# Output strips of a quarter of the columns, and memory rows turned by VectorE, in a segment-recurrent attention block

## The chip, the cores and the metric

The kernel runs on one core of a Trainium2 chip. The metric is device time in microseconds (us) of one execution: the median of three runs, and one further execution is recorded by the hardware profiler. TensorE multiplies matrices, VectorE (DVE in the profile), ScalarE (ACT) and GpSimd (POOL) work on elements, SyncE (SP) issues DMA transfers.

## The reference

A pre-norm block: recurrent attention with 8 memory rows over segments of 32 tokens, then a feed-forward layer with squared ReLU. Batch 1, 2048 tokens, width 640, 32 heads of 128, feed-forward width 1728, bfloat16.

```python
idx = jnp.arange(L)                       # L = M + seg = 8 + 32
mask = (idx[:, None] < M) | (idx[:, None] >= idx[None, :])
mem = mem0
for s in range(n_seg):                    # 64 segments, one after the other
    h = jnp.concatenate([mem, xs], axis=1)            # xs: layernorm(x) of the segment
    q, k, v = (jnp.einsum('btd,dhe->bhte', h, W) for W in (Wq, Wk, Wv))
    scores = jnp.einsum('bhqe,bhke->bhqk', q, k) * scale
    scores = jnp.where(mask[None, None], scores, -1e9)
    o = jnp.einsum('bhqk,bhke->bhqe', softmax(scores), v)
    o = jnp.einsum('bhte,hed->btd', o, Wo)
    mem = o[:, :M, :]                     # the next segment needs these 8 rows
    outs.append(o[:, M:, :])
h = x + concatenate(outs)
out = h + (relu(layernorm(h) @ w1 + b1) ** 2) @ w2 + b2
```

## The kernel before

The 64 segments form a recurrence: step s cannot project its memory rows before step s-1 has produced them. A step works on 32 main rows (8 memory rows and the first 24 tokens, HD = 24) of all heads; the last 8 tokens of each segment ("tails", TL = 8) are projected ahead, four segments at a time, as filler work.

All matmuls of the loop use TensorE as four strips of 32 columns, each with a weight load of its own: four matmuls in a row write the four groups of 32 PSUM partitions. `proj` (L194) projects the 32 rows with 512 columns a matmul: 40 matmuls each for q, k and v in a step.

The order on TensorE is the order in which `step` (L368) writes it:

1. q, k, q, k projections (L450 to L470), with copies by ScalarE and 32 x 32 transposes by VectorE (`flip`, L224) into `qT` and `kT`. `kT` has 64 columns for a head: 32 main keys, and the 8 tail keys four times over, once for each of the four heads that share a group of score rows.
2. `scores(0)` (L401): memory rows against all keys for half of the heads. A mask matmul (L404) first writes -1e9 where a tail key belongs to another head, and 16 matmuls of 64 columns (L409) add the scores. `qz` holds the memory queries spread out with zeros, so that four heads accumulate into one tile.
3. The v projection in pieces, with `token_scores(0)`, `scores(1)` and `token_scores(1)` between them. Token scores (tile `sk`, L485, 40 columns) start with a causal mask by matmul (L481).
4. `soft1` and `soft2` (L413, L422): maximum, exponential, reciprocal, scaling and transpose for the memory rows, on VectorE and ScalarE.
5. One filler unit, then `token_values` of step s-1 and `values` of the memory rows, into tile `po`; `values_out` moves the memory rows to `oT`.
6. Two filler units, then the output product `wo_rounds` (L229): 64 matmuls of 320 columns. Strip j = 2 kh + ch holds half ch of the output columns for half kh of the heads. `wo_out` (L239) adds the two halves of the heads: ScalarE copies partitions 64 to 127 (L243), VectorE adds (L244), and `o` holds 64 rows of 320.
7. Five filler units, then `mem_to_hT` (L304): 20 matmuls against the identity (L308) turn the 8 memory rows so that the width lies on partitions, and VectorE copies them into `hT4` (L310), from which the next step's q projection reads. `tails_in` (L312) brings the next segment's tail queries and keys into `qT` and `kT`, on GpSimd.
8. The remaining filler.

The token softmax (L522 to L539) runs beside the output product: maximum, difference and sum on VectorE, exponential on ScalarE, two products on GpSimd (`pkt`, `pk`), two transposes on VectorE at the step's end; its result is used by the next step's `token_values`.

Filler units come from lists (`fill`): a tail projection unit has 4 matmuls of 512 columns (10 units a step in most steps); every fourth step the 10 units are instead the tail rows' output product (`wo_tail_units`, L285). In a few steps the list is short or empty. `late`, `mid` and `win` hold work of other engines, such as layer norm, for set places. PSUM has three `mm` tiles, one `ch` tile (scores, output product and turned memory rows take turns in it) and the `po` tile.

Of the kernel before, what the change touches and what calls it, by code (L numbers as in the profile page):

```python
# [16 lines left out]
def kernel(  # L17
# [16 lines left out]
    nc = tc.nc  # L34
# [9 lines left out]
    DH = D // 2  # L44
    NB = S // 128
# [36 lines left out]
    mask = const.tile([128, HG, SEG], BF16)  # L82
    nc.vector.memset(mask[:], 0.0)
    nc.gpsimd.affine_select(out=mask[0:32], in_=mask[0:32], compare_op=ALU.is_ge, fill=NEG, base=0,
                            pattern=[[0, HG], [-1, SEG]], channel_multiplier=1)
    bmask = const.tile([128, 4, TL], BF16)
# [10 lines left out]
    nc.vector.tensor_scalar(out=bmask[:], in0=same[:], scalar1=-1.0, scalar2=-NEG, op0=ALU.add, op1=ALU.mult)  # L97
    qT = const.tile([128, H, NK], BF16)
    kT = const.tile([128, H, 2 * SEG], BF16)
# [28 lines left out]

    o_ring = [const.tile([128, DH], BF16, name="o%d" % k) for k in range(5)]
    for o in o_ring:  # L130
        nc.gpsimd.memset(o[64:128], 0.0)
    o0 = o_ring[-1]
    nc.vector.memset(o0[0:64], 0.0)
    load_x(0)
    for ch in range(2):
        nc.sync.dma_start(out=o0[32 * ch:32 * ch + M, :].rearrange("m (c f) -> m c f", f=64),
                            in_=A_mem0[0].rearrange("m (c t f) -> t m c f", t=2, f=64)[ch])
# [89 lines left out]
    wov2 = wo[:].rearrange("p h (c t f) -> p h t c f", t=2, f=64)  # L227

    def wo_rounds(lhs, pw, h0, h1):  # L229

        for h in range(h0, h1):
            for kh in range(2):
                for ch in range(2):
                    j = kh * 2 + ch
                    p = h // 8 * 16 + kh * 8 + h % 8
                    nc.tensor.matmul(pw[32 * j:32 * j + 32, 0:DH], lhsT=lhs(p), rhs=wov2[:, head(p), ch],  # L236
                                     start=(h == 0), stop=(h == 15))

    def wo_out(pw):  # L239
        o = o_ring[0]  # L240
        o_ring.append(o_ring.pop(0))
        tmp = s1.tile([128, DH], F32, tag="tk", name="otmp")
        nc.scalar.copy(out=tmp[0:64], in_=pw[64:128, 0:DH])  # L243
        nc.vector.tensor_tensor(out=o[0:64], in0=pw[0:64, 0:DH], in1=tmp[0:64], op=ALU.add)  # L244
        return o
# [39 lines left out]
    def wo_tail_units(b):  # L285
        st = {}

        def out():
            o = wo_out(st["ps"])
            dst = o_all[:].rearrange("(b s t) d -> b s t d", s=4, t=SEG)  # L290
            for ch in range(2):
                nc.sync.dma_start(out=dst[b, :, HD:SEG, ch * DH:(ch + 1) * DH], in_=o[32 * ch:32 * ch + 32, :])

        def unit(k):
            def f():
                if k == 0:
                    st["ps"] = mmtile()
                wo_rounds(lambda p: oTts[b % 2][:, p, :], st["ps"], k * 16 // 10, (k + 1) * 16 // 10)
                if k == 9:
                    late.append(out)  # L300
            return f
        return [unit(k) for k in range(10)]

    def mem_to_hT(o, hT4, sp):  # L304
        pm = chn.tile([128, 512], F32, tag="ch", name="pm")
        for c in range(DC):
            for q in range(4):
                nc.tensor.matmul(pm[32 * q:32 * q + 32, c * M:(c + 1) * M], lhsT=o[:, (2 * c + q % 2) * 32:(2 * c + q % 2 + 1) * 32],  # L308
                                 rhs=ident[:, q // 2 * 32:q // 2 * 32 + M], start=True, stop=True)
        nc.vector.tensor_copy(out=hT4[:, :, sp, 0:M], in_=pm[:, 0:DC * M].rearrange("p (c m) -> p c m", m=M))  # L310

    def tails_in(b, sp):  # L312
        q, k = [tails[b][w][:].rearrange("p h (k s) -> p h s k", s=4)[:, :, sp, :] for w in "qk"]
        nc.gpsimd.tensor_copy(out=qT[:, :, SEG:NK], in_=q)
        nc.gpsimd.tensor_copy(out=kT[:, :, SEG:2 * SEG].rearrange("p h (j k) -> p h j k", k=TL),  # L315
                              in_=k.unsqueeze(2).to_broadcast([128, H, 4, TL]))
# [11 lines left out]
    def store_main(o, s):  # L328
        for ch in range(2):
            nc.sync.dma_start(out=o_all[s * SEG:s * SEG + HD, ch * DH:(ch + 1) * DH],  # L330
                              in_=o[32 * ch + M:32 * ch + 32, :])
# [36 lines left out]
    def step(b, sp, v=None):  # L368
# [32 lines left out]
        def scores(n):  # L401
            sm = chn.tile([128, 512], F32, tag="ch", name="sm")
            for g in range(G):
                nc.tensor.matmul(sm[32 * g:32 * g + 32, SEG:2 * SEG], lhsT=ident[:, 0:32],  # L404
                                 rhs=bmask[:].rearrange("p j k -> p (j k)"), start=True, stop=False, skip_group_check=True)
            for j in range(4):
                for g in range(G):
                    p = n * 16 + g * 4 + j
                    nc.tensor.matmul(sm[32 * g:32 * g + 32, 0:2 * SEG], lhsT=qz[:, p, :], rhs=kT[:, p, :],  # L409
                                     start=False, stop=(j == 3), skip_group_check=True)  # L410
            sms[n] = sm

        def soft1(n):  # L413
            mx = s2.tile([128, 1], F32, tag="mx", name="mx")
            nc.vector.tensor_reduce(out=mx[:], in_=sms[n][:, 0:2 * SEG], op=ALU.max, axis=AX.X, negate=True)  # L415
            em = s2.tile([128, 2 * SEG], BF16, tag="em", name="em")
            zm = s2.tile([128, 1], F32, tag="zm", name="zm")
            nc.scalar.activation(out=em[:], in_=sms[n][:, 0:2 * SEG], func=ACT.Exp, bias=mx[:, 0:1], scale=1.0,  # L418
                                 accum_out=zm[:])
            ems[n], zms[n] = em, zm  # L420

        def soft2(n):  # L422
            rm = s2.tile([128, 1], F32, tag="rm", name="rm")
            nc.vector.reciprocal(out=rm[:], in_=zms[n][:])
            pm = s2.tile([128, 2 * SEG], BF16, tag="pmem", name="pmem")
            nc.vector.tensor_scalar(out=pm[:], in0=ems[n][:], scalar1=rm[:, 0:1], scalar2=None, op0=ALU.mult)
            pT = s2.tile([128, 2 * SEG], BF16, tag="pTm", name="pTm")
            nc.vector.transpose(out=pT[:], in_=pm[:])
            return pT
# [42 lines left out]
        if not ready:  # L472
            ps0 = mmtile()
            proj(wv, "half", lhs, 0, ps0, 0, 2)
        sk = mmtile()
        skv = sk[:, 0:HG * NK].rearrange("p (i k) -> p i k", k=NK)

        def token_scores(n):
            if n == 0:
                for g in range(G):  # L480
                    nc.tensor.matmul(skv[32 * g:32 * g + 32, :, M:NK], lhsT=ident[:, 0:32], rhs=mask[:],  # L481
                                     start=True, stop=False, skip_group_check=True)
            for j in range(4):
                for g in range(G):
                    nc.tensor.matmul(skv[32 * g:32 * g + 32, n * 4 + j, :], lhsT=qT[:, n * 16 + g * 4 + j, M:NK],  # L485
                                     rhs=kT[:, n * 16 + g * 4 + j, 0:NK], start=False, stop=(n == 1 and j == 3),
                                     skip_group_check=True)

        token_scores(0)
        if not ready:  # L490
            proj(wv, "half", lhs, 0, ps0, 2, DC)
            nc.scalar.copy(out=v[:, 0:512], in_=ps0[:])  # L492
        if not last:
            pT0 = soft2(0)
        if not ready:
            ps1 = mmtile()
            proj(wv, "half", lhs, 1, ps1, 0, 2)
        if not last:
            scores(1)
        token_scores(1)  # L500
        if not ready:
            proj(wv, "half", lhs, 1, ps1, 2, DC)
# [4 lines left out]
        if not ready:  # L507
            nc.scalar.copy(out=v[:, 512:1024], in_=ps1[:])
        run(fill, 10 if ready else 1)
# [13 lines left out]
        nc.vector.tensor_reduce(out=mxk[:], in_=skv, op=ALU.max, axis=AX.X)  # L523
        tk = s1.tile([128, HG, NK], F32, tag="tk", name="tk")
        nc.vector.tensor_tensor(out=tk[:], in0=skv, in1=mxk[:].unsqueeze(2).to_broadcast([128, HG, NK]), op=ALU.subtract)  # L525
        ek = s1.tile([128, HG, NK], BF16, tag="ek", name="ek")
        nc.scalar.activation(out=ek[:], in_=tk[:], func=ACT.Exp, scale=1.0)  # L527
        for f in outs:
            f()
        zk = s1.tile([128, HG], F32, tag="zk", name="zk")  # L530
# [9 lines left out]

        pw = chn.tile([128, 512], F32, tag="ch", name="pw")
        wo_rounds(lambda p: oT[:, p, 0:32], pw, 0, 16)
# [5 lines left out]
        if not last:  # L548
            run(fill, 5)
            mem_to_hT(o, hT4s[(s + 1) // 4], (s + 1) % 4)  # L550
            tails_in((s + 1) // 4, (s + 1) % 4)
# [69 lines left out]
    def prep_sum(t, k, got):  # L621
        ot, fx = got
        fv = fx.rearrange("p (c t f) -> p t c f", t=2, f=64)
        nc.vector.tensor_tensor(out=fv, in0=ot.rearrange("p (t c f) -> p t c f", t=2, f=64), in1=fv, op=ALU.add)
# [81 lines left out]
    mem_to_hT(o0, hT4s[0], 0)  # L706
# [54 lines left out]
    def end_output(s):  # L761
        pw = chn.tile([128, 512], F32, tag="ch", name="pw")
        wo_rounds(lambda p: oT[:, p, 0:32], pw, 0, 16)
# [108 lines left out]
```

## Time and profile before

| | |
|---|---|
| median of 3 runs | 1040.74 us (1040.04 to 1044.46) |
| span of the profiled execution, first to last instruction | 1035.5 us |
| mean granted TensorE clock | 0.993 |
| from the first q projection of step 1 to that of step 63 | 70.18 to 886.12 us |
| TensorE matmuls, busy | 26960, 980.1 us (95%) |
| VectorE, ScalarE, GpSimd busy | 621.6, 536.0, 312.3 us |
| output product L236 of the steps | 4224 matmuls, 300 ns mean |
| turning the memory rows L308 | 1280 matmuls |

A busy time is the union of the instructions' intervals on one engine. Matmuls are pipelined: the mean of one is its whole passage, while four strips start within some nanoseconds of each other, so a stretch of matmuls is read from its start times. In a group, "out<-in" names the tiles, the shape is partitions x elements, and the idle time is that of the engine before the group's instructions, with what ended it; "issue" means that nothing the profile shows was waited for. The median lies 5.2 us above the span.

### The profile page before, as it was taken

Reading aid. Unit: us, or ns where it says so; the run is one execution under the profiler, and the core shown is the slowest. Engines: PE = TensorE matmul, PEld = TensorE weight load, DVE = VectorE, ACT = ScalarE, POOL = GpSimd, SP = SyncE. Lnnn points to the kernel's source line nnn. Section 1 sums busy time; section 2 is a strip of 40 time slices with the busy share of each in tenths; the row PEclk is TensorE's granted clock in tenths of the full one; section 3 lists DMA queues with packets and bytes.
Section 4 is the critical chain, followed back from the end, with each engine's and each line's share of the span. In section 5 each row is a group of like instructions: output and inputs, shape, how many; then the busy total and the mean of one; then the engine's idle time right before and its main releaser. Section 6 shows DMA issues by size and latency. Waiting matters only on the chain.

```text
span 1035.5 us, 58905 instructions
## 1 busy us (share of the span) xinstructions
PE 980.1 (95%) x26960; PEld 563.9 (54%) x26960; DVE 621.6 (60%) x1740; ACT 536.0 (52%) x1225; POOL 312.3 (30%) x805
## 2 busy tenths in 40 slices
PE   5879899999999999999999999999999998999998
PEld 2335455555655555555555655555555555555565
DVE  2155666766566666666666666666666676565432
ACT  2435555555555555555555555555555555534431
POOL 1033333333333333332333233333333333343210
PEclk9889999999999999999999999999999999999999
DMA  8960101000100000000000000000000110612200
GB/s 319 405 205 26 22 7 31 7 24 6 32 10 22 15 24 24 16 20 14 26 15 22 15 27 15 22 15 27 15 21 8 47 33 7 194 54 72 77 26 26
DMA packets 39112, 51.58 MB, mean 50 GB/s; under 512 B 6160, under 2 KB 34960, under 8 KB 36944
## 3 DMA queue, kind: packets, MB, share of 16 engines
q1 hardware_dynamic: 38000, 47.30, 13.8%
q8 instruction: 210, 3.44, 1.4%
q14 instruction: 38, 0.31, 0.1%
q10 hardware_dynamic: 544, 0.26, 0.1%
q0 software_dynamic: 320, 0.26, 0.1%
HBM read 38.37 MB, written 9.44 MB: 46 GB/s over the span
## 4 chain that ended last, share of the span: by engine, by line
PE 83%; DMA 6%; DVE 5%; issue 3%; ACT 2%; POOL 0%; SPq 0%; DVEq 0%; ACTq 0%; POOLq 0%
PE ps L204 45%; PE pw L236 13%; PE y L823 6%; PE ps L791 5%; PE ps L236 3%; DMA xt<-in_A_x_dram 3%; PE po L437 2%; PE pm L308 2%; PE sm L409 2%; DMA wq<-in_B_w_dram 1%; PE po L343 1%; PE ps L485 1%; ACT em L418 1%; DMA vt_d<-row 1%; DVE o L244 1%
## 5 line engine op out<-in xcount | busy, mean ns | idle before, releaser
L204 PEld LDWEIGHTS <-hT 128*32 128x32 bf16 x7680 | 186.9, 96 | 180.8 <-DVE hT L310 19.6
L204 PE MATMUL ps<-wv,hT 128*32 128x512 bf16 x2520 | 169.9, 379 | 0.7 <-ACT v L492 0.7
L236 PE MATMUL pw<-wo,oT 128*32 128x320 bf16 x4224 | 159.6, 300 | 3.3 <-DVE pTt L555 1.2
L204 PE MATMUL ps<-wq,hT 128*32 128x512 bf16 x2520 | 158.1, 380 | 4.8 <-DVE hT L310 4.8
L204 PE MATMUL ps<-wk,hT 128*32 128x512 bf16 x2520 | 157.6, 379 | 0.0
L236 PEld LDWEIGHTS <-oT 128*32 128x32 bf16 x4224 | 109.3, 97 | 50.7 <-DVE oT L211 15.8
L535 POOL TENSOR_TENSOR pkt<-ek,rk 128x64 bf16<-128x64 bf16 x64 | 18.8, 294 | 377.6 <-DVE rk L533 377.6
L220 ACT ACTIVATE row<-ps 128x512 bf16<-128x512 f32 x156 | 91.9, 601 | 78.4 <-PE ps L204 74.6
L225 DVE STREAM_TRANSPOSE qT<-row 128x512 bf16<-128x512 bf16 x128 | 90.6, 709 | 51.9 <-ACT row L220 51.9
L222 ACT CAST row<-ps 128x512 bf16<-128x512 f32 x115 | 65.9, 596 | 34.3 <-PE ps L204 34.3
L315 POOL COPY kT<-kTt 128x1024 bf16<-128x1024 bf16 x64 | 70.9, 1108 | 13.7 <-DVE kTt L225 13.7
L362 POOL COPY qz<-qT 128x96 bf16<-128x96 bf16 x126 | 33.4, 265 | 125.0 <-DVE qT L225 121.5
L353 ACT CAST oT<-po 128x512 bf16<-128x512 f32 x128 | 68.7, 589 | 1.6
L244 DVE TENSOR_TENSOR o<-pw,otmp 64x320 bf16<-64x320 f32 x66 | 31.8, 482 | 61.9 <-ACT otmp L243 61.9
L204 PEld LDWEIGHTS <-hTt 128*32 128x32 bf16 x1920 | 48.8, 99 | 35.6 <-issue 9.9
L225 DVE STREAM_TRANSPOSE kT<-row 128x512 bf16<-128x512 bf16 x65 | 46.0, 708 | 31.1 <-ACT row L222 31.1
L243 ACT COPY otmp<-pw 64x320 f32<-64x320 f32 x66 | 27.9, 422 | 70.9 <-PE pw L236 70.9
L823 PE MATMUL y<-wq,wk 128*128 128x320 bf16 x416 | 60.9, 299 | 0.0
L393 ACT CAST row<-ps 128x256 bf16<-128x256 f32 x126 | 40.7, 375 | 29.1 <-PE ps L204 29.0
L531 DVE TENSOR_REDUCE zk<-ek 128x8 f32<-128x320 bf16 x64 | 31.1, 486 | 40.2 <-ACT ek L527 40.2
L527 ACT ACTIVATE ek<-tk 128x320 bf16<-128x320 f32 x64 | 30.1, 470 | 45.1 <-DVE tk L525 45.1
L418 ACT ACTIVATE em<-sm,mx 128x64 bf16<-128x64 f32 x126 | 40.4, 321 | 24.3 <-DVE mx L415 24.3
(114 smaller groups left out, 1657.5 us busy)
## 6 DMA issues: line engine op xcount, KB each, us to landing
wv<-in_A_Wv_dram SPq DMA_DIRECT2D x5, 1024.0 KB
wq<-in_A_Wq_dram SPq DMA_DIRECT2D x5, 1024.0 KB
wk<-in_A_Wk_dram SPq DMA_DIRECT2D x5, 1024.0 KB
wo<-in_A_Wo_dram SPq DMA_DIRECT2D x4, 1280.0 KB
vt<-vt_d SPq DMA_DIRECT2D x60, 64.0 KB
xt<-in_A_x_dram SPq DMA_DIRECT2D x20, 160.0 KB
vt_d<-row SPq DMA_DIRECT2D x22, 128.0 KB
wq<-in_B_w_dram SPq DMA_DIRECT2D x1, 2080.0 KB
```

The source lines that it names most:

```text
L204: nc.tensor.matmul(ps[32 * k:32 * k + 32, :], lhsT=lhs(c), rhs=wr[:, c, n, k], start=(c == 0), stop=(c == DC - 1))
L220: nc.scalar.mul(out=row, in_=ps, mul=scale)
L222: nc.scalar.copy(out=row, in_=ps)
L225: nc.vector.transpose(out=dst[:, n * 16:(n + 1) * 16, 0:32], in_=row.rearrange("p (h e) -> p h e", e=32))
L236: nc.tensor.matmul(pw[32 * j:32 * j + 32, 0:DH], lhsT=lhs(p), rhs=wov2[:, head(p), ch], start=(h == 0), stop=(h == 15))
L244: nc.vector.tensor_tensor(out=o[0:64], in0=pw[0:64, 0:DH], in1=tmp[0:64], op=ALU.add)
L315: nc.gpsimd.tensor_copy(out=kT[:, :, SEG:2 * SEG].rearrange("p h (j k) -> p h j k", k=TL), in_=k.unsqueeze(2).to_broadcast([128, H, 4, TL]))
L353: nc.scalar.copy(out=oTg[:, n, :, :, M:NK], in_=po[:, :, n * 128:(n + 1) * 128].rearrange("p g (j q) -> p g j q", q=32))
L393: nc.scalar.copy(out=row[:, u * 256:(u + 1) * 256], in_=ps[:, u * 256:(u + 1) * 256])
L418: nc.scalar.activation(out=em[:], in_=sms[n][:, 0:2 * SEG], func=ACT.Exp, bias=mx[:, 0:1], scale=1.0, accum_out=zm[:])
L791: nc.tensor.matmul(ps[:], lhsT=w1[:, c, fc * 128:(fc + 1) * 128], rhs=hnT[:, c, :], start=(c == 0), stop=(c == DC - 1))
L823: nc.tensor.matmul(y[:, hh, 0:DH], lhsT=f1T[:, fc, k * 128:(k + 1) * 128], rhs=w2[:, fc, cs], start=(fc == 0), stop=False, skip_group_chec ...
```

## The change

- The output product is cut into four strips of 160 columns (`DQ`), one for each quarter of the output columns, over all 32 heads: 128 matmuls of 160 columns in place of 64 of 320. The sum of two halves falls away: `wo_out` is one ScalarE copy of 128 x 160. Stores of `o` become four DMAs in place of two, and `prep_sum` reads the new column order.
- `mem_to_hT` is a VectorE transpose of the product in PSUM (float32, 128 x 160) and a copy of 40 columns into `hT4`. It and `tails_in` stand right behind the output product, ahead of the token softmax's sum; all remaining filler comes later. For step 0 the memory rows are turned by 5 matmuls.
- The token mask is no longer written by matmul (L481): VectorE adds it to the scores ahead of the maximum, which adds one operation of 128 x 320.
- `kT` has 40 columns a head: tail keys are held once. The mask matmul L404 falls away, scores of the memory rows have 40 columns, and `soft2` spreads the tail probabilities with a second VectorE operation (a product with `same`).
- Token scores of both halves stand behind the v projection, and `scores(1)` behind its first 24 matmuls instead of the first 28.

```diff
-    def wo_rounds(lhs, pw, h0, h1):
-
-        for h in range(h0, h1):
-            for kh in range(2):
-                for ch in range(2):
-                    j = kh * 2 + ch
-                    p = h // 8 * 16 + kh * 8 + h % 8
-                    nc.tensor.matmul(pw[32 * j:32 * j + 32, 0:DH], lhsT=lhs(p), rhs=wov2[:, head(p), ch],
-                                     start=(h == 0), stop=(h == 15))
+    wov4 = wo[:].rearrange("p h (c q f) -> p h q c f", q=4, f=32)
+    def wo_rounds(lhs, pw, p0, p1):
+        for p in range(p0, p1):
+            for q in range(4):
+                nc.tensor.matmul(pw[32 * q:32 * q + 32, 0:DQ], lhsT=lhs(p), rhs=wov4[:, head(p), q],
+                                 start=(p == 0), stop=(p == H - 1))
     def wo_out(pw):
...
-        nc.scalar.copy(out=tmp[0:64], in_=pw[64:128, 0:DH])
-        nc.vector.tensor_tensor(out=o[0:64], in0=pw[0:64, 0:DH], in1=tmp[0:64], op=ALU.add)
+        nc.scalar.copy(out=o[:], in_=pw[:, 0:DQ])
...
-    def mem_to_hT(o, hT4, sp):
+    def mem_to_hT(pw, hT4, sp):
+        tr = s1.tile([128, DQ], F32, tag="tr", name="tr")
+        nc.vector.transpose(out=tr[:], in_=pw[:, 0:DQ])
+        nc.vector.tensor_copy(out=hT4[:, :, sp, 0:M], in_=tr[:].rearrange("p (c r) -> p c r", r=32)[:, :, 0:M])
...
-        nc.gpsimd.tensor_copy(out=kT[:, :, SEG:2 * SEG].rearrange("p h (j k) -> p h j k", k=TL),
-                              in_=k.unsqueeze(2).to_broadcast([128, H, 4, TL]))
+        nc.gpsimd.tensor_copy(out=kT[:, :, SEG:NK], in_=k)
...
         def scores(n):
             sm = chn.tile([128, 512], F32, tag="ch", name="sm")
-            for g in range(G):
-                nc.tensor.matmul(sm[32 * g:32 * g + 32, SEG:2 * SEG], lhsT=ident[:, 0:32],
-                                 rhs=bmask[:].rearrange("p j k -> p (j k)"), start=True, stop=False, skip_group_check=True)
             for j in range(4):
                 for g in range(G):
                     p = n * 16 + g * 4 + j
-                    nc.tensor.matmul(sm[32 * g:32 * g + 32, 0:2 * SEG], lhsT=qz[:, p, :], rhs=kT[:, p, :],
+                    nc.tensor.matmul(sm[32 * g:32 * g + 32, 0:NK], lhsT=qz[:, p, :], rhs=kT[:, p, :],
...
-            nc.vector.tensor_scalar(out=pm[:], in0=ems[n][:], scalar1=rm[:, 0:1], scalar2=None, op0=ALU.mult)
+            nc.vector.tensor_scalar(out=pm[:, 0:SEG], in0=ems[n][:, 0:SEG], scalar1=rm[:, 0:1], scalar2=None, op0=ALU.mult)
+            nc.vector.scalar_tensor_tensor(out=pm[:, SEG:2 * SEG].rearrange("p (j k) -> p j k", k=TL),
+                                           in0=ems[n][:, SEG:NK].unsqueeze(1).to_broadcast([128, 4, TL]),
+                                           scalar=rm[:, 0:1], in1=same[:], op0=ALU.mult, op1=ALU.mult)
...
-        token_scores(0)
         if not ready:
-            proj(wv, "half", lhs, 0, ps0, 2, DC)
+            proj(wv, "half", lhs, 0, ps0, 0, DC)
...
-            proj(wv, "half", lhs, 1, ps1, 0, 2)
+            proj(wv, "half", lhs, 1, ps1, 0, 1)
         if not last:
             scores(1)
-        token_scores(1)
         if not ready:
-            proj(wv, "half", lhs, 1, ps1, 2, DC)
+            proj(wv, "half", lhs, 1, ps1, 1, DC)
...
+        for i in range(HG):
+            for g in range(G):
+                p = i // 4 * 16 + g * 4 + i % 4
+                nc.tensor.matmul(skv[32 * g:32 * g + 32, i, :], lhsT=qT[:, p, M:NK], rhs=kT[:, p, 0:NK],
+                                 start=(i == 0), stop=(i == HG - 1), skip_group_check=True)
...
-        nc.vector.tensor_reduce(out=mxk[:], in_=skv, op=ALU.max, axis=AX.X)
-        nc.vector.tensor_tensor(out=tk[:], in0=skv, in1=mxk[:].unsqueeze(2).to_broadcast([128, HG, NK]), op=ALU.subtract)
+        nc.vector.tensor_tensor(out=tk[:], in0=skv, in1=mask[:].unsqueeze(1).to_broadcast([128, HG, NK]), op=ALU.add)
+        nc.vector.tensor_reduce(out=mxk[:], in_=tk[:], op=ALU.max, axis=AX.X)
+        nc.vector.tensor_tensor(out=tk[:], in0=tk[:], in1=mxk[:].unsqueeze(2).to_broadcast([128, HG, NK]), op=ALU.subtract)
...
+        pw = chn.tile([128, 512], F32, tag="ch", name="pw")
+        wo_rounds(lambda p: oT[:, p, 0:32], pw, 0, H)
+        if not last:
+            mem_to_hT(pw, hT4s[(s + 1) // 4], (s + 1) % 4)
+            tails_in((s + 1) // 4, (s + 1) % 4)
...
-        pw = chn.tile([128, 512], F32, tag="ch", name="pw")
-        wo_rounds(lambda p: oT[:, p, 0:32], pw, 0, 16)
         o = wo_out(pw)
...
-        if not last:
-            run(fill, 5)
-            mem_to_hT(o, hT4s[(s + 1) // 4], (s + 1) % 4)
-            tails_in((s + 1) // 4, (s + 1) % 4)
         run(mid, 2)
         run(fill, 100)
```

## The prediction

> **What bounds the kernel now.** I read the page first, then the chain of waits, then TensorE's timeline, then the instruction queue.
>
> ```profile
> PE 980.1 (95%) x26960; PEld 563.9 (54%) x26960; DVE 621.6 (60%) x1740; ACT 536.0 (52%) x1225; POOL 312.3 (30%) x805
> ...
> q8 instruction: 210, 3.44, 1.4%
> ```
>
> TensorE looks full. The second line, from the table of DMA queues, matters more than it seems: 3.44 MB in 210 packets is 16,384 bytes a packet, and 2 x 26960 instructions over 210 packets is 257 each. So TensorE's program arrives in blocks of 256 instructions, which is 128 pairs of weight load and matmul.
>
> The end of a step, from the chain of waits (start, duration, what):
>
> ```profile
> 329.15 2.27 PE pw L236 x64
> ...
> 331.49 0.43 ACT otmp L243
> ...
> 331.94 0.49 DVE o L244
> ...
> 332.48 0.35 PE pm L308 x20
> ...
> 332.86 0.21 DVE hT L310
> ...
> 333.12 4.50 PE ps L204 x80
> ```
>
> The output product begins at 329.02 by the timeline, and the next q projection at 333.12: 4.10 us. The same distance is 4.09 us where 28 filler matmuls lie in it (354.83 to 358.92), and in most steps. So a dependency sets it: 2.18 us of streaming and 1.9 us through ScalarE, VectorE, TensorE and VectorE.
>
> The timeline of TensorE shows a second limit (start, duration, group, idle time before):
>
> ```profile
> 288.55 0.45 PE L236 MATMUL pw<-wo,oT 128*32 128x320 bf16 x5
> 289.25 2.22 PE L236 MATMUL pw<-wo,oT 128*32 128x320 bf16 x59 [0.25 <-issue]
> 291.17 1.37 PE L204 MATMUL ps<-wq,hTt 128*32 128x512 bf16 x20
> ```
>
> Five output matmuls run, TensorE stops, and 59 follow; nothing in the profile is waited for. I numbered the matmuls from the start of the trace. Between 165 and 800 us there are 31 pauses of over 60 ns inside a run of like matmuls; 29 come at number 94 plus a multiple of 128, a block's first pair. Each ends 1.2 to 1.6 us (mean 1.41) after a packet of the instruction queue has landed, and the next packet starts 1.0 to 1.65 us after the pause. For the pause above, packets ran 286.80 to 287.73 and 290.28 to 291.57. No packet is fetched two blocks ahead. So a block can begin no sooner than about 3.5 us after the one before: the lowest spacing of packets in the loop is 3.32, a tenth are below 3.49, and two pauses in a row (419.46 and 422.93) lie 3.47 apart. TensorE runs out when it issues 128 pairs in less time.
>
> [...]
>
> From the first q projection at 70.18 to that at 886.12 us lie 62 steps, 815.9 us with 24,895 pairs: 35 steps of 400 pairs (mean 13.05 us), 14 of 424 to 429 that carry a tail output product (13.42), 11 of 360 to 385 with little filler (13.07) and two of 397 (13.85). Undisturbed steps take 12.85.
>
> **The change if only dependencies and streaming counted.** (a) Streaming of the output product: 20 matmuls of 512 columns take 1.09 us and 64 of 320 take 2.18, so 54.5 and 34.1 ns each, about 0.107 ns per column. 160 columns give 17.3 ns, and 128 of them 2.22 us: +0.04 x 82 products, +3. The 64-byte runs of the new weight view cost nothing by the rows: the q projection reads such runs, the v projection long ones, both at 1.09 per 20.
>
> (b) Its end. The copy L243 (0.42), the sum L244 (0.48), 20 matmuls L308 and the copy L310 (0.20) become one VectorE transpose of 160 float32 columns and one copy of 40. No row has that transpose. Below: 0.34, by the bfloat16 transposes (64 columns 0.245, 256 columns 0.42). Above: 0.71, the 512-column transpose. I take 0.4, nearest the 160-column size with something for PSUM; the copy is 0.2 by L310. The distance from product to projection becomes 2.5 + 0.4 + 0.2 + 0.05 = 3.15 us (3.1 to 3.5), or 2.22 + 1.51 = 3.73 where 28 fillers stand in it, 3.81 with tail outputs. Against 4.09 (4.12): -0.36 x 35, -0.31 x 14, -0.9 x 13, in all -29.
>
> (c) Scores to values. In the timeline the second values group starts 8.05 us after the q projection whether a filler is present or not, 3.72 after the first scores, although TensorE could be there at 7.9: the softmax chain sets it. So the mask matmuls removed (L481 0.11, L404 0.02 twice) gain nothing there, and token scores moved later only fill a wait. VectorE stood idle 0.25 for the second scores (L415), which now come about 0.4 earlier. Against that each soft2 gains an operation with a pointer scalar: 0.15 if pipelined as transposes L555 and L561 are (0.16 apart), 0.27 if it waits as L426 to L428 do. 64 to 40 columns saves 0.02 in L415 and in L418. Sum: 8.05 becomes 7.94 (7.85 to 8.18), -0.1 x 62, -7.
>
> (d) Work with cover. The added mask sum (0.49 like L525) delays the exponential to about 2.0 us after the product's start, which ends at 2.5. The sums L531 and L533 now stand behind the transpose, so POOL's pk ends near 4.7 us instead of 3.2; the flips of tail rows wait behind pTt and pTk, and push the first q flip by 0.6 but not the second (0.36 and 0.38 idle before L225's next two). Without that slack it would cost those 0.6. Token values read pTk some 7 us later. On POOL, tails_in goes ahead of pkt, which waits 5.9 us a step (377.6 over 64); its key copy shrinks from 1.11 to 0.43. SP issues two more stores, 0.35 each, and waits 10.5 us a step for L244 (654.1 over 62). Start: that key copy is on the chain before the first values (55.03 in the chain), -0.7; the closing products, +0.
>
> Sum of (a) to (d): -34 us; the step would fall to about 12.4 us with filler.
>
> **The change with the blocks.** Per step: L308 -20 pairs, L404 -8, L481 -4, the product +64: +32, so 400 becomes 432. A tail output product adds 64 more: 429 becomes 525. Pairs of 54 ns (projections and filler) are slow enough: 128 last 7 us. The others are dense: 128 of the new output matmuls last 2.2 us, and the stretch from second scores to values holds 148 pairs in about 2.2. I count the 54-ns stretch by its duration, all other pairs by 3.47 us per 128, and take 0.8 off once, since a block's fetch starts early while slow pairs run (0.1 to 0.6 us after the block's first pair there, 1.19 after a pause).
>
> Before, as a test: 108 x 0.054 + 292/128 x 3.47 - 0.8 = 12.95 (measured 13.05). With tail outputs 80 x 0.054 + 349/128 x 3.47 - 0.8 = 12.98 (13.42). The kernel stands at the point where both limits meet.
>
> After: 5.83 + 324/128 x 3.47 - 0.8 = 13.82 for 35 steps; 4.32 + 445/128 x 3.47 - 0.8 = 15.58 for 14; about 4.5 + 318/128 x 3.47 - 0.8 = 12.3 for 11; 4.32 + 381/128 x 3.47 - 0.8 = 13.85 for two. Sum 484 + 218 + 135 + 28 = 865, so +49 on 815.9; start -0.7, so +48. With 3.32 per block the loop is 839 (+23); with 3.70, the sum of the means 1.19 + 1.10 + 1.41, 904 (+88), but 3.70 would already give 13.5 for steps that measure 13.05. The savings of (b) and (c) vanish: they turn into waits for the program.
>
> The profiled span is 1035.5 us; the median is 1040.74, so 5.2 lies around it. 1040.7 + 48 = 1089.
>
> [...]
>
> **Rivals.** 1. Fetch stays hidden: the pauses come from something else, or the fetch runs further ahead under load. Then the step is bound by (a) to (d): 1040.7 - 34 = 1007, to 1026 if transpose and soft2 stand at their upper ends. For it: the loop's 218 blocks need only 754 us at 3.47, and most packets today are not waited for. Against it: the 29 pauses and the packet that always starts after the block. It decides if 128 pairs can be had in under about 2.9 us. Chance 0.11.
>
> 2. Fetch binds, but credit between slow and dense stretches is larger, so that each step keeps part of its savings: 3.32 per block and 1.2 us of credit give 820, about 1044. For it: spacing has been 3.32. Against: the same numbers give 12.2 for today's steps, 0.6 below their floor. Chance 0.05, spread around no change.
>
> 3. Each of the small matmuls has a floor of its own. Sixteen token-score matmuls start within 0.09 to 0.12 us (L485), 6 to 7 ns each, so 17 ns is far off a floor. [...] Chance 0.02.
>
> **How the numbers follow.** Forecast 0.82: 1089, its own range 1064 to 1115. The whole range reaches down to 1050 for part of rival 2; it leaves out rival 1 and about 0.07 above. Below 0.5%, some 5 us, a measurement of this kernel can't tell a difference; faster is rival 1 and a little of 2 (0.12), same 0.03, slower 0.85.
>
> **What would show it.** Right: some 236 packets on the instruction queue (about 30,200 matmuls), at about 3.5 us in most of the loop; "issue" pauses every 128 pairs, many in L236; tail-output steps near 15.5 us, others near 13.8; TensorE's waits for hT and o gone. Wrong: packets below 3.2 us apart, no pauses in the output product, or a 128-matmul product that streams in 3 us without pauses.

## The result, and the profile after

The changed kernel takes 1123.77 us (median; 1122.58 to 1126.16) against 1042.29 us of the kernel before in the same comparison: ratio 1.0789, 95% interval 1.0769 to 1.0808. It is slower, as forecast, but by 81 us, not 48. The profiled execution spans 1124.4 us at a mean granted clock of 0.979. The loop, from the first q projection of step 1 to that of step 63, takes 897.5 us in place of 815.9, so all of the loss lies there.

The page, engines first, then the instruction queue (packets, MB, share), then the last chain's shares by engine:

```profile
PE 983.8 (87%) x30173; PEld 663.8 (59%) x30173; DVE 656.5 (58%) x1910; ACT 516.3 (46%) x1225; POOL 261.7 (23%) x803
...
q8 instruction: 236, 3.87, 1.5%
...
PE 62%; DVE 17%; issue 11%; DMA 4%; ACT 4%; POOL 1%; ACTq 0%; SPq 0%; DVEq 0%; POOLq 0%
```

There are 3213 more matmuls and 26 more packets, as forecast. TensorE's share fell from 95 to 87 per cent, while its work hardly changed: it waits more. For what, the list of waits of the changed kernel says, weight loads first, then matmuls (engine, line, what it waited for: us in total, times, longest):

```profile
PEld L230 <- issue: 79.7, 75, 3.3
...
PE pw L230 <- issue: 47.1, 53, 3.1
PE ps L230 <- issue: 17.7, 14, 1.6
PE po L432 <- issue: 12.7, 12, 1.7
```

"issue" is a wait for nothing that the profile shows. It sits in the output product (L230, `pw`), in the tail rows' product (L230, `ps`) and in the values (L432). Before, the matmul waits of this kind came to 4.4 us in all; now they are 90.4.

The chain of waits shows one step's end (start, duration, what), the answer to the chain of before:

```profile
341.27 1.03 PE pw L230 x58
342.31 0.88 issue
343.18 1.42 PE pw L230 x70
```

ScalarE's copy, VectorE's sum and the turning matmuls are gone from this place, and a hole in the product has come in their stead. In a step with a tail output product the timeline shows three such holes:

```profile
161.68 0.29 PE L432 MATMUL po<-pTm,v 32*128 32x8 bf16 x16
161.82 0.18 PE L437 MATMUL po<-pTm,vt 32*128 32x32 bf16 x1
163.09 0.19 PE L437 MATMUL po<-pTm,vt 32*128 32x32 bf16 x3 [1.10 <-issue]
...
164.15 1.49 PE L230 MATMUL pw<-wo,oT 128*32 128x160 bf16 x76
166.55 1.08 PE L230 MATMUL pw<-wo,oT 128*32 128x160 bf16 x52 [0.91 <-issue]
167.46 1.49 PE L230 MATMUL ps<-wo,oTt 128*32 128x160 bf16 x76
170.55 0.46 PE L230 MATMUL ps<-wo,oTt 128*32 128x160 bf16 x16 [1.61 <-issue]
```

Between the second and the third lie 52 + 76 = 128 matmuls, one block of the program. Packets of the instruction queue landed at 161.64, 165.22 and 169.07 us, each 1.3 to 1.5 us ahead of the end of a hole.

By kind of step (mean us, forecast in brackets): 35 steps of 432 pairs 14.10 (13.82); 13 of 525 pairs 16.13 (15.58); 11 with little filler 13.5 (12.3), single ones from 12.4 to 16.1.

### The profile page after: what moved, and what is told of

It reads as the page before. It is cut to its first block, busy times and chain, and to the rows that moved or that the text cites. A ratio compares the mean times of both kernels' runs of the same rounds, so it can differ in the third digit from the quotient of the medians.

```text
span 1124.4 us, 66026 instructions
## 1 busy us (share of the span) xinstructions
PE 983.8 (87%) x30173; PEld 663.8 (59%) x30173; DVE 656.5 (58%) x1910; ACT 516.3 (46%) x1225; POOL 261.7 (23%) x803
## 3 DMA queue, kind: packets, MB, share of 16 engines
q1 hardware_dynamic: 43680, 47.30, 12.8%
## 4 chain that ended last, share of the span: by engine, by line
PE 62%; DVE 17%; issue 11%; DMA 4%; ACT 4%; POOL 1%; ACTq 0%; SPq 0%; DVEq 0%; POOLq 0%
PE ps L201 29%; PE pw L230 15%; PE ps L775 5%; PE y L807 5%; DVE kT L391 3%; PE ps L230 3%; DMA xt<-in_A_x_dram 3%; DVE pmem L419 2%; DVE pTm L423 2%; DVE pmem L418 2%; ACT em L410 2%; PE po L432 2%; ACT row L388 1%; DVE rm L416 1%; DVE qT L222 1%
## 5 line engine op out<-in xcount | busy, mean ns | idle before, releaser
L201 PEld LDWEIGHTS <-hT 128*32 128x32 bf16 x7680 | 244.6, 96 | 149.9 <-issue 16.1
L230 PE MATMUL pw<-wo,oT 128*32 128x160 bf16 x8448 | 180.2, 240 | 49.7 <-issue 47.1
L230 PEld LDWEIGHTS <-oT 128*32 128x32 bf16 x8448 | 157.2, 100 | 77.5 <-issue 58.9
L201 PE MATMUL ps<-wv,hT 128*32 128x512 bf16 x2520 | 160.1, 380 | 0.0
L298 DVE STREAM_TRANSPOSE tr<-pw 128x160 f32<-128x160 f32 x63 | 22.1, 350 | 140.3 <-PE pw L230 140.3
L201 PEld LDWEIGHTS <-hTt 128*32 128x32 bf16 x1920 | 56.6, 99 | 39.6 <-issue 18.2
L236 ACT CAST o<-pw 128x160 bf16<-128x160 f32 x66 | 19.3, 293 | 127.2 <-DVE tr L298 114.2
L230 PE MATMUL ps<-wo,oTt 128*32 128x160 bf16 x2048 | 47.8, 235 | 17.7 <-issue 17.7
L210 ACT CAST oT<-po 128x128 bf16<-128x128 f32 x63 | 16.8, 267 | 101.0 <-DVE oT L208 101.0
L401 PEld LDWEIGHTS <-qz 128*32 128x32 bf16 x2016 | 39.4, 95 | 37.6 <-POOL qz L357 8.1
L432 PE MATMUL po<-pTm,v 32*128 32x8 bf16 x2016 | 36.0, 166 | 23.4 <-issue 12.7
```

The lines of the kernel that those rows point to most:

```text
L201: nc.tensor.matmul(ps[32 * k:32 * k + 32, :], lhsT=lhs(c), rhs=wr[:, c, n, k], start=(c == 0), stop=(c == DC - 1))
L230: nc.tensor.matmul(pw[32 * q:32 * q + 32, 0:DQ], lhsT=lhs(p), rhs=wov4[:, head(p), q], start=(p == 0), stop=(p == H - 1))
L401: nc.tensor.matmul(sm[32 * g:32 * g + 32, 0:NK], lhsT=qz[:, p, :], rhs=kT[:, p, :], start=(j == 0), stop=(j == 3))
L432: nc.tensor.matmul(po[:, g, c0 + j * M:c0 + (j + 1) * M], lhsT=v[r, i * E:(i + 1) * E], rhs=pT[r, j * M:(j + 1) * M], start=(s == 0 and i ...
```

## The experiments

Ratios are to the kernel before in the same comparison; I turn them into us with 1040. Four kernels were run first: two that split the change in its halves, one that takes the added matmuls away at equal streaming time, and one that measures the block by itself.

**same_stream: fewer pairs, the same streaming.**

```diff
-        for p in range(p0, p1):
+        for p in range(p0 // 2, p1 // 2):
             for q in range(4):
-                nc.tensor.matmul(pw[32 * q:32 * q + 32, 0:DQ], lhsT=lhs(p), rhs=wov4[:, head(p), q], ...)
+                nc.tensor.matmul(pw[32 * q:32 * q + 32, 0:DH], lhsT=lhs(p), rhs=wov2[:, head(p), q % 2], ...)
```

> The changed kernel, but each output product takes only 16 of its 32 heads, with 320 columns a matmul: 64 matmuls that stream as long (2.18 us) as the 128 of 160 columns did (2.22 us), with every copy, transpose and order of the change as it was. Half of the heads is left out of the output. Steps have 368 pairs in place of 432. Program fetch (about 3.5 us or a little more for each 128 pairs): the blocks no longer bind, and what is left is the sum of dependencies and streaming, 1007 to 1030 us. A VectorE chain or the new order as the cause: nothing that it needs is taken away, so 1124 as before. [...]

Measured: 1029.46 us, ratio 0.9863 (0.9820 to 0.9906). 94 us go with 64 matmuls a product that take no more streaming time in sum. That leaves no room for VectorE's chain or the order as the main cause. It is the upper end of what program fetch promised, 22 above the forecast's own sum.

**ladder: the price of a block.**

```diff
+    for wdt in (8, 160, 256, 320):
+        lp = chn.tile([128, 512], F32, tag="ch", name="lp")
+        for i in range(768):
+            j = i % 4
+            nc.tensor.matmul(lp[32 * j:32 * j + 32, 0:wdt], lhsT=oT[:, i % H, 0:32], rhs=hnT0[:, i // 4 % DC, 0:wdt], ...)
```

> The kernel before with four runs of 768 matmuls behind its last projection, with 8, 160, 256 and 320 columns, which wait for nothing (the output is not touched). Time of 128 pairs within a run. Program fetch: 3.5 to 3.7 us with 8 and with 160 columns alike, about the same at 256 (streaming alone is 3.5 there), 4.4 at 320. Streaming at 0.107 ns a column alone: 0.9, 2.2, 3.5, 4.4 us. [...]

The timeline of its end (start, duration, group, idle time before):

```profile
1036.71 1.28 PE L845 MATMUL lp<-hnT,oT 128*32 128x8 bf16 x141
1038.83 1.17 PE L845 MATMUL lp<-hnT,oT 128*32 128x8 bf16 x128 [0.84 <-issue]
1042.58 1.19 PE L845 MATMUL lp<-hnT,oT 128*32 128x8 bf16 x128 [2.57 <-issue]
1046.05 1.19 PE L845 MATMUL lp<-hnT,oT 128*32 128x8 bf16 x128 [2.28 <-issue]
1049.80 1.19 PE L845 MATMUL lp<-hnT,oT 128*32 128x8 bf16 x128 [2.56 <-issue]
1053.54 1.88 PE L845 MATMUL lp<-hnT,oT 128*32 128x8 bf16 x128 [2.56 <-issue]
1057.01 9.60 PE L845 MATMUL lp<-hnT,oT 128*32 128x160 bf16 x384 [1.59 <-issue]
1067.70 2.40 PE L845 MATMUL lp<-hnT,oT 128*32 128x160 bf16 x128 [1.09 <-issue]
1071.17 2.40 PE L845 MATMUL lp<-hnT,oT 128*32 128x160 bf16 x128 [1.07 <-issue]
1074.91 2.85 PE L845 MATMUL lp<-hnT,oT 128*32 128x160 bf16 x128 [1.35 <-issue]
```

Here nothing else can be waited for, and with 8 and 160 columns TensorE stops every 128 matmuls, but for one stretch. Starts are 3.75, 3.47, 3.75, 3.74 and 3.47 us apart with 8 columns, 3.47 and 3.74 with 160; from 1038.83 to 1082.13 us, over the first three widths, 12 blocks took 43.30 us, 3.61 each. The stretch without holes, 384 matmuls from 1057.01 us, begins at half the clock: from 1057.0 to 1062.9 us the granted clock was 0.51, four matmuls of 160 columns took 0.133 us instead of 0.069, and streaming lasted as long as the fetch. Between 8 and 160 columns width plays no part. With 256 columns the two limits can't be told apart: after a last hole at 1082.13 us, four blocks in a row took 3.49 us each, which is about what 128 x 256 columns need to stream (3.5 by the prediction's 0.107 ns a column). So 3.61 is a mean and not a floor. With 320 columns streaming is slower than the fetch (26.0 us, 4.33 a block) and the holes are gone. The first hole comes only after 141 matmuls, 13 more than a block: the rest of one block and one whole block were in hand. The fetch is not hidden here: from the second hole on, 2.3 to 2.6 us of each block of 8-column matmuls are a wait.

**e1_parts and e2_strips: the two halves of the change.** e2_strips has the quarter-column strips, the turning by VectorE and the place of the product's end; e1_parts has the edits of mask, tail keys, soft2 and token scores. Both together are the changed kernel.

```diff
# e2_strips: wov4, mem_to_hT by VectorE, its place behind the product, four stores
-        wo_rounds(lambda p: oT[:, p, 0:32], pw, 0, 16)
+        wo_rounds(lambda p: oT[:, p, 0:32], pw, 0, H)
# e1_parts: mask added by VectorE; kT of 40 columns, soft2 in two; token scores behind the v projection
-    kT = const.tile([128, H, 2 * SEG], BF16)
+    kT = const.tile([128, H, NK], BF16)
-        token_scores(0)
```

> The kernel before with all of the change but the strips and the turning: mask added by VectorE, tail keys once, soft2 in two operations, token scores behind the value projection. 388 pairs a step in place of 400. Program fetch: no slower, 1020 to 1042 us. VectorE's longer softmax chain, or the moved token scores, as the cause of the slowdown: slower than before, by 0.2 us a step (1053) if in part, up to 1124 if alone.

> The kernel before with only the quarter-column strips, the turning by VectorE and the place of the product's tail: the mask matmuls stay, so 444 pairs a step. Program fetch: the whole slowdown and some of the 12 pairs more a step (0.33 us at 3.5 us for 128), 1115 to 1150 us. If VectorE's softmax chain was the cause: 1007 to 1040.

Measured: e1_parts 1063.59 us, ratio 1.0229 (1.0184 to 1.0273); e2_strips 1109.72, ratio 1.0659 (1.0640 to 1.0677). The strips cost 69 us, for which the theory of program fetch had an explanation: numbering the matmuls, 87 of 98 pauses in runs of like matmuls between 70 and 880 us come at number 94 plus a multiple of 128, and those 87 sum to 60.7 us beyond the streaming. They are not the only cost in e2_strips. Matmul waits of the kind "issue" come to 57.0 us in all, but the largest line among the matmul waits is another, for the memory rows' softmax:

```profile
PE po L433 <- DVE pTm L424: 30.8, 56, 0.8
```

There the scaling in the later `soft2` (L422) lasts 825 ns in the mean, against 242 before. It ends 33 to 46 ns after GpSimd's copy of tail keys (L311, 1.09 us), which overlaps it in all of the loop's steps and in none of the kernel before; the product starts 9.31 us after the q projection at best, in place of 8.75. That is up to 0.56 x 62 = 35 us, and the savings of the shorter end stand against it.

And e1_parts went against the theory: 24 us slower with 12 pairs a step fewer. The rival, VectorE's longer chain, had forecast just that. Its waits spoke for a third reading:

```profile
PE po L436 <- issue: 12.7, 13, 1.5
...
PE pw L236 <- issue: 5.1, 13, 1.6
...
PE po L441 <- issue: 4.8, 4, 1.2
```

These are waits for the program again, now ahead of the values (L436, L441) and in the product. The new theory, clumping: the 32 token-score matmuls, which had stood among slow matmuls of the value projection, now stand in one run with the values and the output product, so that more of a block's boundaries fall where the program can't keep up. Two kernels tell it from VectorE's chain:

**ts_moved and e1_keep: the move alone, and all but the move.**

```diff
# ts_moved, against the kernel before
-        token_scores(0)
...
-        token_scores(1)
...
             nc.scalar.copy(out=v[:, 512:1024], in_=ps1[:])
+        token_scores(0)
+        token_scores(1)
```

> The kernel before with one move: both halves of the token scores, with their mask matmuls, stand in one run behind the value projection instead of among its matmuls. 400 pairs a step as before, no work added on any engine. Program fetch with clumping (the 36 quick pairs no longer lie among slow ones, so more blocks fall wholly into quick work): slower by most of what e1_parts lost or more, 1055 to 1080 us. VectorE's longer softmax chain as the cause of e1_parts' loss: no change, 1036 to 1046.

> e1_parts with the token scores and the second scores left at their places of before: mask added by VectorE, tail keys once, soft2 in two operations, 388 pairs a step. Clumping: no slower than before, 1020 to 1042 us. VectorE's chain: slower like e1_parts, 1055 to 1070.

Measured: ts_moved 1050.72 us, ratio 1.0113 (1.0086 to 1.0140); e1_keep 1037.60, ratio 0.9971 (0.9953 to 0.9988). The same instructions in another order cost 12 us, less than I expected; in e1_keep everything VectorE was given costs nothing. In ts_moved, the pauses in runs that stand at 94 plus a multiple of 128 went from 29 (9.1 us) to 42 (22.4 us) between 70 and 880 us. In e1_parts the move costs 1063.6 - 1037.6 = 26 us, and matmul waits of the kind "issue" are 26.7 us there against 5.3 in e1_keep. So the rival falls for these kernels. The move of e1_parts also has the second scores four matmuls earlier, which ts_moved has not; how much of the step from 12 to 26 us that makes, no run shows.

**after_keep: the move undone in the changed kernel.** Token scores and second scores stand among the value projection's matmuls; the rest is as changed.

```diff
-            proj(wv, "half", lhs, 0, ps0, 0, DC)
+            proj(wv, "half", lhs, 0, ps0, 0, 2)
...
+        token_scores(0)
+        if not ready:
+            proj(wv, "half", lhs, 0, ps0, 2, DC)
```

> The changed kernel with the token scores and the second scores back among the value projection's matmuls, as before the change; all else as changed, 432 pairs a step. If the clumping of quick pairs is a cost of its own in the changed kernel too: 1095 to 1112 us. If the number of pairs alone decides: 1120 to 1127, as the changed kernel.

Measured: 1092.40 us, ratio 1.0519 (1.0496 to 1.0542), a little under what clumping promised. Its waits, beside those of the changed kernel above:

```profile
PE pw L230 <- issue: 46.4, 52, 3.5
PE ps L230 <- issue: 16.6, 14, 1.6
...
PE po L432 <- issue: 2.8, 5, 1.2
```

The waits in the products are the same (46.4 and 47.1, 16.6 and 17.7). Those ahead of the values fall from 12.7 to 2.8, and weight loads there (L432) from 29.2 to 6.6 us, while weight loads ahead of the token values (L338) rise from 9.7 to 20.6. By the ratios the move costs 28 us of the changed kernel's 82; the loops differ by 897.5 - 869.8 = 27.7. All matmul waits for the program together fall by 90.4 - 76.7 = 13.7 us, so they are about half of it.

Another part is on VectorE. The timeline of the changed kernel, at the end of the second `soft2` (start, duration, group, idle time before):

```profile
325.09 0.42 POOL L310 COPY qT<-qTt 128x256 bf16<-128x256 bf16 x1 [1.99 <-PE ps L491]
325.09 0.46 DVE L419 SCALAR_TENSOR_TENSOR pmem<-em,rm,same 128x32 bf16<-128x32 bf16 x1
...
325.45 0.40 POOL L311 COPY kT<-kTt 128x256 bf16<-128x256 bf16 x1
...
325.59 0.24 DVE L423 STREAM_TRANSPOSE pTm<-pmem 128x64 bf16<-128x64 bf16 x1
325.89 0.26 PE L432 MATMUL po<-pTm,v 32*128 32x8 bf16 x16 [0.20 <-DVE pTm L423]
```

GpSimd's copies for the next step (`tails_in`) wait for the token scores (L491) and start 7.40 us after the q projection (median), in after_keep 6.69. In the changed kernel they fall on VectorE's operation L419, which lasts 428 ns in the mean of the second `soft2`, against 250 in after_keep; in 59 of 63 cases it ends 43 to 63 ns after one of the copies. The product then starts 8.81 us after the q projection at best, in after_keep 8.67: 0.14 us, about 9 us if it counts in all 62 steps. No run takes this part from the move by itself.

**same_keep: neither blocks nor move.** This is same_stream with the token scores back in place.

> same_stream with the token scores and the second scores back among the value projection's matmuls: 64 output matmuls of 320 columns a product (half of the heads is left out of the output), VectorE's turning, mask and split soft2 as changed, 368 pairs a step. If the sum of dependencies and streaming (-34 us) was right and the rest of the miss is blocks and clumping: 1005 to 1015 us. If the sum was too hopeful: 1025 to 1040, like same_stream (1029).

Measured: 1005.29 us, ratio 0.9659 (0.9634 to 0.9683). The sum of dependencies and streaming was right: -35 us, forecast -34. Of the kernels with the new end of the product, it is the one with the fewest matmul waits for the program (8.0 us). Two by two, in us against the kernel before:

| | 64 matmuls a product | 128 matmuls a product |
|---|---|---|
| token scores among the value projection | -35 (same_keep) | +54 (after_keep) |
| token scores behind it | -14 (same_stream) | +82 (the change) |

The added matmuls cost 89 to 96, the move 21 to 28. The lower row holds GpSimd's collision with `soft2` as well (in the second `soft2`, L420 of same_stream lasts 429 ns, of same_keep 250).

**dense40 and sparse40: a test that didn't tell.** Forty matmuls of 8 columns were added to each step, in one run behind the output product, or two and two among the q and k projections.

```diff
# dense40
+        for i in range(40):
+            nc.tensor.matmul(pw[32 * (i % 4):32 * (i % 4) + 32, 480:488], lhsT=ident[:, 0:32], rhs=ident[:, 0:8], ...)
# sparse40, behind each four matmuls of a q or k projection
+                for i in range(2):
+                    j = (2 * c + i) % 4
+                    nc.tensor.matmul(extra["t"][32 * j:32 * j + 32, 480:488], lhsT=ident[:, 0:32], rhs=ident[:, 0:8], ...)
```

> The kernel before with 40 more matmuls of 8 columns behind each output product, 0.3 us of TensorE's time at the pace of the token scores, in a place where TensorE waits 1.9 us anyway. 440 pairs a step, the output unchanged. Program fetch at 3.61 us for 128 pairs (by the ladder): up to 1.13 us a step, 1085 to 1113 us. Engine time alone: hidden or 0.3 us a step, 1040 to 1060.

> The same 40 matmuls of 8 columns as in dense40, but spread two and two among the matmuls of the q and k projections, which run at 54 ns a pair. 440 pairs a step, the output unchanged. Program fetch: hidden there, only the engine time of 0.3 us, 1040 to 1060 us, against 1071 in dense40. If the number of pairs a step decides wherever they stand: 1065 to 1075 as in dense40.

Measured: 1070.84 us (1.0304, 1.0278 to 1.0331) and 1079.49 us (1.0383, 1.0363 to 1.0403), both outside of what I expected, and sparse40 above dense40 instead of below. Both places were on the path. In sparse40 the first scores start 4.95 us after the q projection in place of 4.36: each added matmul costs 0.59/40 = 15 ns of TensorE's time there, not the 7 that I had reckoned. In dense40 the added ones write the product's own tile, so its copy waits for them; they end the product 0.50 us later, 12 ns each. The kernels show the time of a small matmul on the path, not the fetch, and settle nothing.

**best_keep, best2, best3: fewer pairs.** Adding the two halves of the product while turning them takes 10 matmuls in place of 20 and VectorE's sum off the path; the token scores keep their place.

```diff
+    turn = ...  # [128, 2, M]: ident columns 32 ch + m and 64 + 32 ch + m added
+        nc.vector.tensor_copy(out=ob[:, 0:DQ], in_=pw[:, 0:DQ])      # best_keep; best2: one ScalarE copy
+        nc.scalar.copy(out=ob[:, DQ:DH], in_=pw[:, DQ:DH])
...
+                nc.tensor.matmul(pm[64 * t:64 * t + 64, c * M:(c + 1) * M], lhsT=o[:, c * 64:(c + 1) * 64], rhs=turn[:, t], ...)
...
-            run(fill, 5)
+            run(fill, 4)                                              # best3 alone, one unit ahead of the second values
```

> e1_keep with a shorter end of the product: the two halves are copied to bfloat16 without being added (VectorE 160 columns, ScalarE 160), and 10 turning matmuls of 64 columns against a matrix with two ones a column add them while they turn; GpSimd adds the halves for the store, off the path. 378 pairs a step, product to projection shorter by about 0.5 us. Program fetch and dependencies: 0.5 us x 62, so 1000 to 1022. If the blocks bind already: as e1_keep or above it.

> best_keep with the two halves copied by ScalarE in one operation of 320 columns (0.43 us by the copy of that size before) in place of VectorE's and ScalarE's copies, which ran one after the other (0.33 + 0.29 and the gap). 378 pairs a step. Product to projection 0.2 us shorter than in best_keep: 1022 to 1038 us. If blocks bind at 3.61 us for 128 pairs (5.83 + 270/128 x 3.61 - 0.8 = 12.6 us a step): no lower than 1025.

> best2 with the filler placed anew: in best2 most steps had 20 filler matmuls (1.08 us) between the product and the turning matmuls and 8 behind them, so that the filler and not the copy set the 2.0 us from the last output matmul to the next projection. One unit now stands ahead of the second values and four, not five, behind the product. If filler on the path is what kept best2 from its gain: 0.2 to 0.4 us in most steps, 1015 to 1030 us. If program blocks took it: 1033 to 1040, as best2.

Measured: 1042.55 (1.0029, 1.0011 to 1.0046), 1037.35 (0.9983, 0.9973 to 0.9994) and 1036.58 (0.9986, 0.9974 to 0.9999). In best_keep the two copies of one tile ran one after the other:

```profile
ACT ob L311 <- DVE ob L310: 63.8, 62, 2.1
```

Putting that right brought half a per cent; the filler's place brought no more. e1_keep, best2 and best3 lie 0.1 to 0.3 per cent below the kernel before, less than the half per cent that I called measurable; best_keep lies above it. Waits for the program are no longer what holds them (e1_keep 5.3 us in all on the matmuls, best2 5.4); in one step of best2, at 110 us, the scores wait 4.4 us for GpSimd's `qz` and the step takes 18.2 us in place of 13.6, which alone is 0.4 per cent. Otherwise, why a step that is 0.5 us shorter in its dependencies takes 12.7 us at the least and 13.0 in the mean stays open.

## Why the prediction was right or wrong

**Mechanism, sign and counts: right.** The product streams in 2.2 us and waits for its program; 236 packets, about 30,200 matmuls, holes 128 matmuls apart, waits for `hT` and `o` turned into waits for the program. The packets stood 3.79 us apart in the median of the loop, not "about 3.5 us in most of" it. Rival 1 (fetch stays hidden) is refuted by ladder and same_stream, rival 2 by the time; its sum, by its own numbers, comes to 815 and not 820. Rival 3 (a floor for each small matmul) is refuted by ladder: four matmuls took 0.033 us there with 8 columns and 0.069 with 160, 8 and 17 ns each, and 17 is what 160 columns need by (a).

**The sum (a) to (d), -34 us: right.** same_keep measured -35. Its undisturbed steps show, from product to projection, 3.03 us with no filler between (taken 3.15, the range 3.1 to 3.5), 3.70 with 28 filler matmuls (3.73) and 3.80 with tail outputs (3.81); VectorE's transpose takes 0.350 us (taken 0.4), and the product's first start comes 0.08 us earlier at best (taken 0.1). The added VectorE work was hidden, as e1_keep shows. What (d) missed is that `tails_in`, in its new place, can fall on `soft2`.

**The step that failed: in (c), "token scores moved later only fill a wait".** That term follows neither TensorE's program nor the engines that the token scores release. The block formula took "0.8 off once", wherever a step's quick pairs stand. The move cost 28 us that no term had: 13.7 us are seen as matmul waits for the program, up to about 9 can be `soft2` under GpSimd's copies, and the rest is not assigned. With the token scores in their old place the change measures 1092, and the formula's 1089 would have held, in part by luck: steps of 432 pairs took 13.63 (13.82), of 525 pairs 15.59 (15.58), those with little filler 13.2 (12.3), errors of -7 and +10 us that cancel.

**The price and the credit were both too small, and hid each other.** I took 3.47 us a block because that was the spacing of one pair of pauses, and put 3.70 aside because it gave 13.5 us for steps of the kernel before that measure 13.05. In the changed kernel 36 neighbouring pauses lie 120 to 136 matmuls apart, in three clusters: 12 at 3.45 to 3.48 us, 16 at 3.72 to 3.76, 8 at 4.00 to 4.03; mean 3.71. So 3.70 was the right price for neighbouring blocks, and the credit is what the test should have changed. From the steps with 3.70: after_keep 5.83 + 324/128 x 3.70 - 13.63 = 1.57 and 4.32 + 445/128 x 3.70 - 15.59 = 1.59; the changed kernel 15.20 - 14.10 = 1.10 and 17.18 - 16.13 = 1.05. At that price, two kinds of step agree on a credit of 1.6 us with the token scores among slow matmuls, 1.1 without. That 0.5 x 62 = 31 is near the move's cost is no test, since both come from the same steps. On kernels that it wasn't taken from, the formula fits e2_strips (13.94 against 13.90 us for 444 pairs, 15.93 against 15.70 for 537) and fails with fewer pairs: 12.8 against 13.4 for the 388 of e1_parts, 12.3 against 13.1 for the 368 of same_stream. What the move costs there is not a fixed credit a step; it stays open. With 3.70 and 1.6 a 400-pair step of before comes to 5.83 + 292/128 x 3.70 - 1.6 = 12.7, below its undisturbed 12.85. That is why the test misled: those steps were set by dependencies, and I fitted a fetch model to them.

**The short steps** (12.3 forecast) took 13.5 in the mean. That is 11 x 1.2 = 13 us of the 32.5 by which the loop missed its forecast. A price of 3.70 and a credit of 1.1 would give only 12.6. In one of them, at 110 us, the scores wait 2.0 us for GpSimd's `qz`; the others stay open, and no run looked at them by themselves.

**The range** of 1050 to 1115 had its upper end at 3.70 a block with the wrong credit, cut short by the same test; it would have held after_keep, not the change.

## What to carry to other kernels

Where a stream of matmuls is narrow, count instructions as well as columns: the product cut into twice as many matmuls of half the width streamed as long here (2.2 us), but its program did not arrive in time (47.1 us of matmul waits in it). Quick matmuls are best left among slow ones: moving the token scores out from among them cost 12 us in ts_moved and 28 in the changed kernel, where GpSimd's copies can have a part. That a block fetched during slow work is what the next quick run lives on is my estimate, from credits of 1.6 and 1.1 us a step at 3.70 us a block; no run shows it by itself. Moved work also moves what waits for it: ask which engine it releases, and on what that work then falls. Fit the price of a suspected limit in a place where nothing else can be waited for: a run of blocks at the end of the kernel gave it directly (3.61 us in the mean), while steps that another limit set gave a wrong pair of numbers that fitted (3.47 and 0.8).

## What the runs showed of the hardware

- A block of 256 TensorE instructions came every 3.47 or 3.74 us when nothing else was waited for (ladder; 3.61 in the mean), and at 3.47, 3.74 or 4.02 in the changed kernel: steps of 0.27 us, alike with 8 and with 160 columns. Four blocks of 256 columns came at 3.49.
- In ladder, 141 quick matmuls passed before the first hole, 13 more than the 128 of one block: one block beyond the one in use had been fetched.
- A matmul of 8 columns cost 15 ns among slow matmuls of 512 columns (sparse40), 8 ns (0.033 us for four) in a run of its own (ladder), in a stretch with a mean granted clock of 0.64.
- VectorE turned 128x160 float32 from PSUM in 0.350 us (63 transposes of the changed kernel, mean).
- Where GpSimd's copies fell on the second `soft2`, VectorE's scaling ended 33 to 63 ns after a copy in 122 of 126 cases, and lasted 825 ns in place of 242 (e2_strips) and 428 in place of 250 (changed kernel).
